# The last two token groups of the second mixture: 384 and 128 tokens in place of 256 and 256

## The chip, the cores and the metric

The kernel runs on one core of a Trainium2 chip. Its time is the device time in microseconds (us); a kernel's figure is the median of its runs. TensorE multiplies matrices, VectorE and ScalarE work on elements, GpSimd does some of that and issues gathers and scatters, and SyncE issues most transfers.

## The reference

A decaying linear attention (4 sequences of 768 tokens, 8 heads of 48) gives 3072 tokens of 384 numbers. A first mixture sends each token to one of 8 experts (384 to 1024 to 384). The second mixture, the part that changes, is this for all tokens:

```
h = np.maximum(np.maximum(x @ w1, x @ w2), x @ w3)   # 384 -> 768, three products
return (h @ w_out).astype(np.float32)                # 768 -> 384
```

## The kernel before

Attention comes first, ordered by a planner that is not touched. Then `experts` runs, with an order written out by hand: two loops over steps issue each engine's work in program order, and a table (`at`, `step`) attaches side work (loads, splits, gathers) to step numbers.

Products of the experts and of the second mixture are made with split numbers: each operand is a high part and a low part in the format fp32r, and `three` (lines 719 to 723) issues three products for one: high x high, high x low, low x high. Each is one TensorE instruction with its own load of 128 x 128 weights (the stationary operand), and the moving operand's columns stream through. The smallest number of columns that the kernel gives to such a product is 256.

The second mixture treats its 3072 tokens in groups of sizes `GS` (line 868): five of 512 and two of 256. `group(g)` splits a group's inputs into halves `gh` and `gl`. For each group there are NF = 6 steps, f = 0 to 5, one per 128 of the 768 hidden features:

- `up2(g, f)` makes the three products for 128 features: 3 weights x 3 slices of the inner dimension x 3 split products = 27 instructions, with the weights stationary and the group's G tokens as the moving columns. Each of the three results has a PSUM tile `pqt` of its own, out of four (pool `pq`). ScalarE copies the first into `h` (line 913), VectorE takes the maximum with the second and the third (914, 915), ScalarE makes the high part `hh` and VectorE the low part `hl` (`split`, lines 158 and 161).
- `down2(g, f)` multiplies by the output weights. Here the tokens are stationary, 128 at a time, and 384 output columns move: three instructions for each 128 tokens, added up over the six steps in a PSUM tile `pot` per 128 tokens. At f = 5 each such block is scaled by its gate (`sg`) out of PSUM into `orow`, by ScalarE for even blocks and by VectorE for odd ones, and GpSimd issues an indirect transfer that scatters the 128 rows to the output (line 941). The very last block of the program is halved: VectorE scales one half of its columns, ScalarE the other (lines 933 to 936).

`down2` of a step is issued after `up2` of the next step, so that the elementwise work between them has a whole `up2` to be done in. Only after the last `up2` nothing is left to put in between.

At step N1 + 37, in the last group, a matrix product and a copy make the flag (line 980) by which the program decides whether to run a slower path at the end; it is not taken here.

Of the kernel before, what the change touches and what calls it, by code (L numbers as in the profile page):

```python
# [10 lines left out]
F32 = mybir.dt.float32  # L11
# [3 lines left out]
AF = mybir.ActivationFunctionType  # L15
ALU = mybir.AluOpType
# [5 lines left out]
HD = H * D  # L22
# [132 lines left out]
def split(nc, hi, lo, src, hi_eng=None, lo_eng=None):  # L155

    if hi_eng is None:
        nc.scalar.copy(hi, src)  # L158
    else:
        hi_eng.tensor_copy(hi, src)  # L160
    (lo_eng or nc.vector).tensor_tensor(out=lo, in0=src, in1=hi.bitcast(F32), op=ALU.subtract)  # L161
# [427 lines left out]
def experts(ctx, tc, io, xs, R, ids_d, scale_d, V32):  # L589

    nc = tc.nc
# [12 lines left out]
    pq = ctx.enter_context(tc.tile_pool(name="pq", bufs=4, space=PSUM))  # L604
# [114 lines left out]
    def three(out, st_, mv, start, stop):  # L719
        (sh, sl), (mh, ml) = st_, mv  # L720
        nc.tensor.matmul(out, lhsT=sh, rhs=mh, start=start, stop=False)  # L721
        nc.tensor.matmul(out, lhsT=sh, rhs=ml, start=False, stop=False)  # L722
        nc.tensor.matmul(out, lhsT=sl, rhs=mh, start=False, stop=stop)  # L723

    HH = {}
    ACC = {}
# [14 lines left out]
    def down(e, f):  # L741
        if f == 0:
            ACC[e] = [po.tile([128, 512], F32, tag="po", name="pacc") for _ in range(3)]
        wh, wl = W[8 * e + f // 2 * 2 + 1]
        for m in range(3):
            ms = slice(m * 128, (m + 1) * 128)
            three(ACC[e][m][:, :CAPS[e]], (wh[:, f % 2, ms], wl[:, f % 2, ms]), HH[e, f], f == 0, f == 7)
        if f == 7:
            for m in range(3):
                o = yT[:, m, bass.ds(R["off"][e], CAPS[e]) if e else slice(CAP)]  # L750
                if m == 1:
                    nc.scalar.copy(o, ACC[e][m][:, :CAPS[e]])
                else:
                    nc.vector.tensor_copy(o, ACC[e][m][:, :CAPS[e]])
# [110 lines left out]
    xc.close()  # L865
    gp = ctx.enter_context(tc.tile_pool(name="gp", bufs=2))
    fp = ctx.enter_context(tc.tile_pool(name="fp", bufs=1))
    GS = [512] * 5 + [256] * 2
    G0 = [sum(GS[:g]) for g in range(len(GS))]
    XG = {}  # L870

    def group(g):
        G = GS[g]
        hi = gp.tile([128, 3, G], F32R, tag="gh", name="gh")
        lo = gp.tile([128, 3, G], F32R, tag="gl", name="gl")
        for k in range(3):
            split(nc, hi[:, k], lo[:, k], yT[:, k, G0[g]:G0[g] + G], lo_eng=nc.gpsimd if g else nc.vector)
        XG[g] = (hi, lo)

    group(0)  # L880
    down(*last)
    NG, NF = len(GS), F2 // 128
    ir = fp.tile([B * NC, 128], F32, name="ir", bufs=1)
# [8 lines left out]
    def places(g):  # L892
        for t in range(G0[g] // 128, (G0[g] + GS[g]) // 128):
            ic = gp.tile([128, 1], I32, tag="ic", name="ic", bufs=12)
            nc.vector.tensor_copy(ic, ig[:, t:t + 1])
            sg = gp.tile([128, 1], F32, tag="sg", name="sg", bufs=12)
            nc.gpsimd.indirect_dma_start(out=sg, out_offset=None, in_=scale_d, in_offset=bass.IndirectOffsetOnAxis(ap=ic[:, :1], axis=0),
                                         bounds_check=NT - 1, oob_is_err=False)
            R["ic", t], R["sg", t] = ic, sg

    def up2(g, f):
        G = GS[g]
        xh, xl = XG[g]
        fs = slice(f % 2 * 128, f % 2 * 128 + 128)
        pp = []
        for i in range(3):
            p = pq.tile([128, 512], F32, tag="pq", name="pqt")[:, :G]
            wh, wl = W[N1 + f // 2 * 4 + i]
            for k in range(3):
                three(p, (wh[:, k, fs], wl[:, k, fs]), (xh[:, k], xl[:, k]), k == 0, k == 2)  # L910
            pp.append(p)
        h = gp.tile([128, 512], F32, tag="h2", name="h2", bufs=2)[:, :G]
        nc.scalar.copy(h, pp[0])  # L913
        nc.vector.tensor_tensor(out=h, in0=h, in1=pp[1], op=ALU.max)  # L914
        nc.vector.tensor_tensor(out=h, in0=h, in1=pp[2], op=ALU.max)  # L915
        hi = hp.tile([128, 512], F32R, tag="hh", name="hh")[:, :G]
        lo = hp.tile([128, 512], F32R, tag="hl", name="hl")[:, :G]
        split(nc, hi, lo, h)
        HH[g, f] = (hi, lo)

    def down2(g, f):
        nt = GS[g] // 128
        if f == 0:
            ACC[g] = [po.tile([128, 512], F32, tag="po", name="pot") for _ in range(nt)]
        hh, hl = HH[g, f]
        wh, wl = W[N1 + f // 2 * 4 + 3]
        for t in range(nt):
            ts_ = slice(t * 128, (t + 1) * 128)
            three(ACC[g][t][:, :HD], (hh[:, ts_], hl[:, ts_]), (wh[:, f % 2], wl[:, f % 2]), f == 0, f == NF - 1)
            if f == NF - 1:  # L930
                o = gp.tile([128, HD], F32, tag="o", name="orow", bufs=4)
                n = G0[g] // 128 + t
                if t == GS[-1] // 128 - 1 and g == len(GS) - 1:
                    half = HD // 2
                    nc.vector.tensor_scalar(out=o[:, half:], in0=ACC[g][t][:, half:HD], scalar1=R["sg", n], scalar2=None, op0=ALU.mult)
                    nc.scalar.activation(out=o[:, :half], in_=ACC[g][t][:, :half], func=AF.Copy, scale=R["sg", n])
                elif t % 2:
                    nc.vector.tensor_scalar(out=o, in0=ACC[g][t][:, :HD], scalar1=R["sg", n], scalar2=None, op0=ALU.mult)
                else:
                    nc.scalar.activation(out=o, in_=ACC[g][t][:, :HD], func=AF.Copy, scale=R["sg", n])  # L940
                i = nc.gpsimd.indirect_dma_start(out=io["out"], out_offset=bass.IndirectOffsetOnAxis(ap=R["ic", n][:, :1], axis=0),  # L941
                                                 in_=o, in_offset=None, bounds_check=NT - 1, oob_is_err=False)
                tc.declare_no_dep(i.ins, group="rows", reason="each token has one row")
                tc.add_to_no_dep_group("rows", i.ins)
# [49 lines left out]
    for s in range(NG * NF):  # L994
        now = (s // NF, s % NF)
        up2(*now)
        if last:
            down2(*last)
        last = now
        step(N1 + s)  # L1000
    down2(*last)


# [160 lines left out]
def build(ctx, tc, io):  # L1164
# [26 lines left out]
    for e in range(E):  # L1191
        nc.gpsimd.memset(R["ec"][:, 0, e:e + 1], float(e))
    attention(tc, io["a"], io["qk"], io["v"], io, xs, R)
    experts(tc, io, xs, R, ids_d, scale_d, V32)
    flag = nc.values_load(R["flag"][0:1, 0:1], min_val=0, max_val=128, skip_runtime_bounds_check_because="a count of partitions")
    with tc.If(flag > 0):
# [71 lines left out]
```

## Time and profile before

| | |
|---|---|
| median of 3 runs | 809.87 us (808.35 to 811.32) |
| the profiled execution | 810.14 us |
| its span, first to last instruction | 808.3 us |
| mean granted clock of TensorE | 0.989 |
| TensorE products, weight loads (share of span) | 97%, 87% |
| VectorE, ScalarE, GpSimd | 59%, 49%, 34% |

The profile comes from one execution. A row of the timeline gives the start and the length in us, the engine, the line of the kernel, the operation, what it writes and reads, and in brackets how long the engine was idle before and what released it. PE is TensorE's products, PEld its weight loads, DVE VectorE, ACT ScalarE, POOL GpSimd. Products overlap in the pipeline: a record's length holds latency, so the spacing from one start to the next, and not the length, tells what a product costs in a row of them. Where a row stands for several instructions, its length goes from the first start to the last end. A plain fp32 product leaves two records for each product in the code.

### The profile page before, as it was taken

The page shows a single profiled execution, that of the slowest core. Times are in us where ns is not written, and L with a number is a line of the kernel's source. Part 1 is how long each engine was busy: PE and PEld are TensorE (multiplying, and loading weights), DVE is VectorE, ACT ScalarE, POOL GpSimd, SP SyncE. Part 2 cuts the span into 40 slices and gives each one's busy share as a digit, 9 for nine tenths or more (in the row PEclk, how much of TensorE's full clock was granted, in tenths as well). Part 3 has the DMA queues.
Part 4 walks back from the last instruction along what each step waited for, and adds up shares of the span by engine and source line. Part 5 has one row for each costly group of instructions (what it writes and reads, how often), then busy time and mean ns, then how long its engine had stood idle before and what let it go on. Part 6 is the DMA issues. An engine that isn't in the chain of part 4 may idle for free.

```text
span 808.3 us, 13655 instructions
## 1 busy us (share of the span) xinstructions
PE 784.1 (97%) x5131; PEld 699.9 (87%) x5131; DVE 479.9 (59%) x940; ACT 392.4 (49%) x638; POOL 272.6 (34%) x284
## 2 busy tenths in 40 slices
PE   8999999999996999999999999999999999999995
PEld 6778888888895888999999899888888888888994
DVE  3899999999773565766757543243433434334531
ACT  7989999997931444444445553111211112111211
POOL 1022144231212566655556871121312213112402
PEclk9999999999998999999999999999999999999998
DMA  7852533323115657557577751002102021020200
GB/s 242 262 183 93 165 126 123 128 97 115 56 47 150 210 172 243 193 179 242 192 231 242 245 176 60 1 1 97 59 17 83 0 98 59 20 78 1 99 21 23
DMA packets 59597, 97.63 MB, mean 121 GB/s; under 512 B 7141, under 2 KB 42885, under 8 KB 58501
## 3 DMA queue, kind: packets, MB, share of 16 engines
q1 hardware_dynamic: 55126, 86.96, 33.5%
q0 software_dynamic: 3904, 9.49, 3.1%
q8 instruction: 42, 0.69, 0.4%
q10 hardware_dynamic: 495, 0.25, 0.1%
q14 instruction: 30, 0.25, 0.1%
HBM read 79.64 MB, written 17.00 MB: 120 GB/s over the span
## 4 chain that ended last, share of the span: by engine, by line
PE 84%; issue 5%; DVE 4%; ACT 2%; DMA 2%; POOL 1%; SPq 1%; POOLq 0%; DVEq 0%; ACTq 0%
PE pqt L721 8%; PE pqt L723 8%; PE pqt L722 8%; PE pt L413 5%; PE pt L397 4%; PE php L721 4%; PE php L722 4%; PE php L723 4%; PE pacc L722 4%; PE pacc L723 4%; PE pacc L721 4%; PE ps L445 3%; PE pc L311 3%; PE ps L426 3%; PE pot L721 3%
## 5 line engine op out<-in xcount | busy, mean ns | idle before, releaser
L161 POOL TENSOR_TENSOR wl<-wraw,wh 128x768 fp32r<-128x768 f32 x68 | 132.1, 1950 | 82.8 <-ACT wh L158 72.8
L721 PE MATMUL pqt<-gh,wh 128*128 128x512 f32 (+1 forms) x378 | 136.9, 362 | 0.0
L722 PE MATMUL pqt<-gl,wh 128*128 128x512 f32 (+1 forms) x378 | 136.8, 362 | 0.0
L723 PE MATMUL pqt<-gh,wl 128*128 128x512 f32 (+1 forms) x378 | 136.8, 362 | 0.0
L158 ACT CAST hh<-h 128x512 fp32r<-128x512 f32 (+1 forms) x42 | 23.6, 561 | 153.8 <-DVE h L915 151.6
L914 DVE TENSOR_TENSOR h<-h,pqt 128x512 f32<-128x512 f32 (+1 forms) x42 | 25.7, 612 | 111.5 <-PE pqt L723 91.2
L737 ACT ACTIVATE hh<-php 128x480 fp32r<-128x480 f32 (+7 forms) x64 | 33.1, 517 | 100.5 <-PE php L723 100.3
L723 PEld LDWEIGHTS pqt<-gh,wl 128*128 128x128 f32 x378 | 70.9, 188 | 12.3
L721 PEld LDWEIGHTS pqt<-gh,wh 128*128 128x128 f32 x378 | 70.9, 188 | 11.1
L722 PEld LDWEIGHTS pqt<-gl,wh 128*128 128x128 f32 x378 | 70.9, 188 | 11.0
L738 DVE SCALAR_TENSOR_TENSOR hl<-php,hh 128x480 fp32r<-128x480 f32 (+7 forms) x64 | 37.4, 584 | 68.6 <-ACT hh L737 68.6
L721 PE MATMUL php<-xh,wh 128*128 128x480 f32 (+7 forms) x192 | 69.5, 362 | 0.0
L722 PE MATMUL php<-xl,wh 128*128 128x480 f32 (+7 forms) x192 | 67.7, 353 | 0.0
L723 PE MATMUL php<-xh,wl 128*128 128x480 f32 (+7 forms) x192 | 67.7, 352 | 0.0
L722 PE MATMUL pacc<-hl,wh 128*128 128x480 f32 (+7 forms) x192 | 67.3, 350 | 0.3 <-DVE hl L738 0.3
L723 PE MATMUL pacc<-hh,wl 128*128 128x480 f32 (+7 forms) x192 | 67.1, 350 | 0.0
L721 PE MATMUL pacc<-hh,wh 128*128 128x480 f32 (+7 forms) x192 | 67.0, 349 | 0.0
L158 ACT CAST wh<-wraw 128x768 fp32r<-128x768 f32 x76 | 61.9, 830 | 8.9 <-DMA wraw<-w 8.5
L913 ACT COPY h<-pqt 128x512 f32<-128x512 f32 (+1 forms) x42 | 22.1, 527 | 88.2 <-PE pqt L723 87.2
L941 POOL DMA_INDIRECT out<-orow,ic x24 | 23.8, 991 | 118.1 <-ACT orow L940 112.9
L511 POOL TENSOR_TENSOR run<-run,oh 128x8 bf16<-128x8 bf16 x24 | 9.9, 414 | 157.4 <-DVE oh L488 132.7
L915 DVE TENSOR_TENSOR h<-h,pqt 128x512 f32<-128x512 f32 (+1 forms) x42 | 25.7, 611 | 46.9 <-PE pqt L723 45.3
(168 smaller groups left out, 1833.1 us busy)
## 6 DMA issues: line engine op xcount, KB each, us to landing
wraw<-w SPq DMA_DIRECT2D x64, 384.0 KB
fa<-a SPq DMA_DIRECT2D x8, 1152.0 KB
a<-a SPq DMA_DIRECT2D x11, 768.0 KB
qk<-qk SPq DMA_DIRECT2D x11, 768.0 KB
raw<-v SPq DMA_DIRECT2D x9, 768.0 KB
v<-v SPq DMA_DIRECT2D x11, 512.0 KB
xe<-xs SPq DMA_DIRECT2D x21, 192.5 KB
v<-w SPq DMA_DIRECT2D x9, 384.0 KB
```

What stands on the lines that cost most here:

```text
L158: nc.scalar.copy(hi, src)
L161: (lo_eng or nc.vector).tensor_tensor(out=lo, in0=src, in1=hi.bitcast(F32), op=ALU.subtract)
L311: eng.matmul(d[name, j][:, :HD], lhsT=tri if name == "L" else trit, rhs=d["h" if name == "L" else "t"][:, j], start=True, stop=True)
L397: eng.transpose(d[p, j, g][:96, z * 128:(z + 1) * 128], d[yh, j][:, 4 * g + z].rearrange("p r n -> p (r n)"), idn)
L413: eng.matmul(p[:, z * 128:(z + 1) * 128], lhsT=d["kT", j][:, h], rhs=d["qT", j][:, h], start=True, stop=True)
L721: nc.tensor.matmul(out, lhsT=sh, rhs=mh, start=start, stop=False)
L722: nc.tensor.matmul(out, lhsT=sh, rhs=ml, start=False, stop=False)
L723: nc.tensor.matmul(out, lhsT=sl, rhs=mh, start=False, stop=stop)
L737: nc.scalar.activation(out=hi, in_=p, func=AF.Relu)
L738: nc.vector.scalar_tensor_tensor(out=lo, in0=p, scalar=0.0, in1=hi.bitcast(F32), op0=ALU.max, op1=ALU.subtract)
L914: nc.vector.tensor_tensor(out=h, in0=h, in1=pp[1], op=ALU.max)
L915: nc.vector.tensor_tensor(out=h, in0=h, in1=pp[2], op=ALU.max)
```

## The change

The last two groups have 384 and 128 tokens. In the group of 128, the three products of a step are put into one PSUM tile, side by side, 128 columns each. The last block, now the only one of its group, is scaled as a whole by VectorE; the halves are gone.

```diff
-    GS = [512] * 5 + [256] * 2
+    GS = [512] * 5 + [384, 128]
...
         pp = []
+        whole = pq.tile([128, 512], F32, tag="pq", name="pqt") if G == 128 else None
         for i in range(3):
-            p = pq.tile([128, 512], F32, tag="pq", name="pqt")[:, :G]
+            p = whole[:, i * G:(i + 1) * G] if G == 128 else pq.tile([128, 512], F32, tag="pq", name="pqt")[:, :G]
...
-                if t == GS[-1] // 128 - 1 and g == len(GS) - 1:
-                    half = HD // 2
-                    nc.vector.tensor_scalar(out=o[:, half:], in0=ACC[g][t][:, half:HD], scalar1=R["sg", n], scalar2=None, op0=ALU.mult)
-                    nc.scalar.activation(out=o[:, :half], in_=ACC[g][t][:, :half], func=AF.Copy, scale=R["sg", n])
-                elif t % 2:
+                if t % 2 or g == len(GS) - 1:
                     nc.vector.tensor_scalar(out=o, in0=ACC[g][t][:, :HD], scalar1=R["sg", n], scalar2=None, op0=ALU.mult)
```

## Rows read from the trace of the kernel before

**Rows 1.** The page: busy time by engine; the chain that ended last, by engine.
```profile
PE 784.1 (97%) x5131; PEld 699.9 (87%) x5131; DVE 479.9 (59%) x940; ACT 392.4 (49%) x638; POOL 272.6 (34%) x284
...
PE 84%; issue 5%; DVE 4%; ACT 2%; DMA 2%; POOL 1%; SPq 1%; POOLq 0%; DVEq 0%; ACTq 0%
```

**Rows 2.** Timeline, TensorE: a step of the last group (start us, length us).
```profile
784.57 0.28 PE L721 MATMUL pqt<-gh,wh 128*128 128x256 f32 x1
...
787.72 0.34 PE L721 MATMUL pot<-wh,hh 128*128 128x384 f32 x1
...
788.77 0.28 PE L721 MATMUL pqt<-gh,wh 128*128 128x256 f32 x1
```

**Rows 3.** Timeline, TensorE: the `down2` of a group of 512, first to next.
```profile
734.89 0.34 PE L721 MATMUL pot<-wh,hh 128*128 128x384 f32 x1
...
736.98 0.39 PE L721 MATMUL pqt<-gh,wh 128*128 128x512 f32 x1
```

**Rows 4.** Groups by shape, 640 us to the end: weight loads (busy us, mean ns).
```profile
L723 PEld LDWEIGHTS pqt<-gh,wl 128*128 128x128 f32 x220 | 41.3, 188 | 5.1
```

**Rows 5.** Groups by shape, whole span: products and a load of attention.
```profile
L413 PE MATMUL pt<-qT,kT 96*128 96x128 f32 x384 | 50.8, 280 | 0.0
...
L445 PE MATMUL ps<-v,kh 128*96 128x48 f32 x320 | 29.8, 246 | 0.0
...
L428 PEld LDWEIGHTS ps<-qT,S 96*64 96x64 f32 x320 | 23.1, 137 | 0.0
```

**Rows 6.** Timeline, TensorE: runs of such products (weights 96*128: rows x loaded columns).
```profile
30.96 1.48 PE L445 MATMUL ps<-v,kh 128*96 128x48 f32 x16
...
36.37 1.95 PE L413 MATMUL pt<-qT,kT 96*128 96x128 f32 x16
...
41.99 1.93 PE L471 MATMUL ps<-sel,yT 128*128 128x112 f32 x16
...
153.66 0.44 PE L426 MATMUL ps<-P,v 128*64 128x128 f32 x4
153.88 0.44 PE L428 MATMUL ps<-qT,S 96*64 96x128 f32 x4
```

**Rows 7.** Stretches: busy of PE, PEld, DVE, ACT, POOL; clock, DMA, GB/s.
```profile
157.00:158.90 1.90, 1.90 (x18) 1.90 (x17) 0.94 (x2) 1.90 (x5) 0.00 (x0) 1.00 0.90 323
...
784.57:788.77 4.20, 4.20 (x34) 4.20 (x34) 1.27 (x3) 0.78 (x3) 0.00 (x0) 1.00 0.01 4
```

**Rows 8.** Timeline, all engines: from the last product of `up2` on.
```profile
796.02 0.28 PE L723 MATMUL pqt<-gh,wl 128*128 128x256 f32 x1
...
796.34 0.42 DVE L915 TENSOR_TENSOR h<-h,pqt 128x256 f32<-128x256 f32 x1 [0.56 <-PE pqt L723]
...
797.25 0.44 PE L721 MATMUL pot<-wh,hh 128*128 128x384 f32 x1
...
797.71 0.45 PE L723 MATMUL pot<-wh,hl 128*128 128x384 f32 x1
...
798.20 0.58 ACT L940 ACTIVATE orow<-pot,sg 128x384 f32<-128x384 f32 x1 [1.00 <-PE pot L723]
...
798.72 0.42 DVE L935 TENSOR_SCALAR orow<-pot,sg 128x192 f32<-128x192 f32 x1 [1.06 <-PE pot L723]
799.05 1.01 POOL L941 DMA_INDIRECT out<-orow,ic  x1 [7.11 <-ACT orow L940]
799.17 0.42 ACT L936 ACTIVATE orow<-pot,sg 128x192 f32<-128x192 f32 x1 [0.39 <-DVE orow L935]
800.37 0.99 POOL L941 DMA_INDIRECT out<-orow,ic  x1 [0.30 <-issue]
```

**Rows 9.** Groups by shape, 640 us to the end: elementwise work (busy us, mean ns).
```profile
L914 DVE TENSOR_TENSOR h<-h,pqt 128x512 f32<-128x512 f32 x13 | 9.0, 689 | 40.5 <-PE pqt L723 32.5 <-issue 8.0
...
L913 ACT COPY h<-pqt 128x256 f32<-128x256 f32 x12 | 4.5, 373 | 14.9 <-PE pqt L723 13.8 <-issue 1.0
L938 DVE TENSOR_SCALAR orow<-pot,sg 128x384 f32<-128x384 f32 x7 | 4.1, 611 | 0.2 <-PE pot L723 0.2
```

## The prediction

> **What bounds the kernel now.** I read the engines' busy shares first, then the chain of waits, and both say one thing: TensorE is busy 97% of the span, and 84% of the chain that ended last is its work [rows 1]. So a change in the last stage is worth what it does to TensorE's spacing from one product to the next, plus what it does to the stretch after the last product, where nothing covers anything.
>
> Next the timeline of the last two groups. There a step (one `up2`, one `down2`) is 27 products of 256 columns and then 6 of 384. The 27 take 784.57 to 787.72, that is 3.15 us or 0.1167 each; the 6 take 1.05; the whole step is 4.20 [rows 2]. In the groups of 512 the 12 products of 384 columns take 734.89 to 736.98, 2.09 us or 0.1742 each [rows 3]. So a column costs 0.454 to 0.456 ns at 384 and at 256, and nothing fixed is seen. But every product loads its own 128 x 128 weights first (a load's record is 188 ns, part of it latency) [rows 4], and whether that load still hides under 128 columns is what this case turns on.
>
> **The rate at 128 columns.** The trace has no product of split numbers (fp32r) under 256 columns, so the nearest rows must bound it. In attention, plain fp32 products run with as few columns. 16 of `L471`, 112 columns with a 128-column load, take 1.93 us from first start to last end; with one record of 0.28 taken off, 15 spacings are 0.110 each. 16 of `L413`, 128 columns with a 128-column load, give (1.95 - 0.28) / 15 = 0.111. 16 of `L445`, only 48 columns but a 96-column load, give (1.48 - 0.246) / 15 = 0.082: far above 48 columns' worth, and 0.857 ns per loaded column, which for 128 gives 0.110. From four of `L426` to four of `L428`, whose loads have 64 columns, 0.22 goes by, so 0.055 each, again 0.86 ns per loaded column [rows 5, 6]. Load records shrink from 188 to 137 ns between 128 and 64 columns, 0.80 ns per column [rows 4, 5]. So loads seem to run one behind the other, at about 0.86 ns per column, and 128 columns of weights take 0.110 us however few columns follow. At 256 columns the stream (0.1167) just covers that; at 128 it does not.
> I bound the spacing x below by half of 0.1167 = 0.058 (columns alone) and above by two records of `L413`'s kind, 0.223: a small split product treated as a plain fp32 one, which in attention leaves two records (`scores` issues 192 products in all, 8 heads x 24 blocks, and `L413` shows 384 [rows 5]). I take 0.110, from the two rows with the same load.
>
> **The sum, part by part.**
> *Group of 384 for 256.* 6 steps x 27 = 162 products go from 0.1167 to 0.1742: 162 x 0.0575 = +9.3 us. The elementwise work grows by half, under a step that grows to (27 + 9) x 0.1742 = 6.27 us; ScalarE and VectorE use 0.8 and 1.3 us of a 4.2 us step now [rows 7], so it stays hidden. Uncovered, it would lengthen the way from a step's last maximum to its `down2`, which has a whole `up2` in between.
> *Group of 128 for 256.* 162 products go from 0.1167 to x: 162 x (0.110 - 0.1167) = -1.1 us. With x = 0.058 it would be -9.5, with 0.223 +17.2.
> *Products of `down2`.* 12 per pair of steps before (6 and 6) and after (9 and 3), same columns: 0. They need `hh` and `hl` of the step before; in the small group these come 1.6 and 1.9 us after the start of the last product of their step (worked out below), and 27 x 0.110 = 2.97 us of the next `up2` stand in between. At x = 0.058 that cover is 1.57 us and the 0.5 of an earlier `down2`: just enough.
> *One PSUM tile for three products.* Fewer buffers of `pq` are taken, which frees nothing, since TensorE waits for none now. What it can cost is that the copy of the first product, which now starts after 9 of the 27, must wait for all 27, because the tile that it reads is still being written. The row that bears on it: the two halves of the last scaling, VectorE's and ScalarE's, read one PSUM tile at different columns, and ScalarE's began at 799.17, when VectorE's (798.72 + 0.42) was done, its idle time put down to that [rows 8]. So I reckon with the wait. Queued behind the copy on ScalarE is only the cast of the same step, and behind that nobody but `down2` waits. In steps 0 to 4 the next `up2` hides it; in the last it is on the path.
> *The tail.* Before: the last product of `up2` starts at 796.02, VectorE's second maximum at 796.34; the first output product starts at 797.25, its third, which waits for `hl`, at 797.71; ScalarE's scaling at 798.20; GpSimd issues the two blocks of output rows at 799.05 and 800.37, the second late because the first holds the queue for 1.01 and 0.30 more goes by [rows 8]. After: operations of 128 columns. VectorE's 512-column maximum is 0.689 [rows 9] and its 256-column one 0.42 [rows 8], so 128 are 0.29; ScalarE's copy is 0.373 at 256 [rows 9], so about 0.26. I take 0.29 to 0.30 for cast and difference too, and 0.03 to 0.05 between two, as the rows show. From the start of the last product: its end 0.28, copy 0.32 to 0.58, maxima to 0.91 and 1.21, cast 1.24 to 1.54 (so `hh` is there at about 1.6), difference to 1.86, third output product at 1.92 with a record of 0.45, whole-row scaling on VectorE 2.41 to 3.02 (0.611 [rows 9]), and GpSimd's issue 0.27 behind it at 3.29, as 799.05 stands 0.27 behind 798.20 + 0.58. Before it was 800.37 - 796.02 = 4.35. So -1.1 us; from -0.4 (if the operations are no shorter than at 256 columns) to -1.7 (no wait for the shared tile). What follows the last issue, the rows' landing and the end of the program, is the same.
> *The rest.* Gathers of the scales and splits of `yT`: as many tokens, issued steps ahead, on GpSimd, which idles for whole steps [rows 7]: 0. The flag of the recurrence still comes two steps into the last group, now some 20 us before the end: 0.
>
> Sum: +9.3 - 1.1 - 1.1 = +7.1 us. The profiled execution took 810.14 (span 808.3 and 1.8 around it), so 817.2; the median of the runs shown is 0.27 lower, which makes 817.0. With x from 0.107 to 0.117 and the tail's bounds, 816 to 819.
>
> **Rivals.**
> *A, small split products lose their single pass.* The chip could run an fp32r product of 128 columns as it runs a plain one, in two records: x = 0.223, +9.3 + 17.2 - 1.1 = +25.4, 835.3. For it: no product of that format under 256 columns is in the trace to exclude it. Against it: the cost per column is the same from 384 to 256 [rows 2, 3], with no sign of a step.
> *B, the load hides after all (the other side: not slower).* If loads are pulled far enough ahead, x = 0.058: +9.3 - 9.5 - 1.1 = -1.3, 808.6, no change that can be told. The place is the spacing in the last six steps; it decides below x = 0.066, where 162 x (x - 0.0592) equals the tail's 1.1. For it: `L426` and `L428` do run 128 columns every 0.055. Against it: they load 64 columns, and `L445` shows that few columns do not speed up a wide load [rows 6].
> *C, something between.* If fp32r weights load faster than fp32 ones, and 128 columns come at the spacing that `L445` reaches with 96, 0.082: 162 x 0.0228 = +3.7 - 1.1 = +2.6, 812.5. For it: nothing but that the formats differ; against it: their records are as long (188 ns here; 0.110 and 0.111 at the two rows with a 128-column load). The Trainium skill has nearly that figure (TensorE: Matmul & The Clock Gate, "Back-to-back issue gap"): in a sustained stream of load and product pairs, about 81 ns for one of 128 columns. By that rule the time would be 812.3; `L413` and `L471`, at 0.111 and 0.110, do not agree with it, which is why it gets little.
> *D, the clock.* In the small group the array streams columns about half the time, and the granted clock may fall from 2.4 to 1.2 GHz. If all there took twice as long, x would be 0.22 and the time about 835. Against it: in attention's stretch of `L471`, just as bound by loads, the granted clock is 1.00 [rows 7].
>
> **How the numbers follow.** The forecast 0.63 (816 to 819), A 0.17, D 0.04, C 0.07, B 0.07, and 0.02 for a stall in the larger group's steps that I don't see. A measurement of this kernel can tell 0.3%, 2.4 us, from no change. Slower: forecast, A, D, the stall, and over half of C = 0.90; same: nearly all of B and the rest of C = 0.08; faster: 0.02. The range leaves out B and C and holds the rest: 814 to 837. The likeliest case's own is 816 to 819.
>
> **What would show it.** In the changed profile, the spacing of `pqt` in the last group: 0.110 is the forecast, 0.058 B, 0.082 C, 0.22 A or (at a lower granted clock) D. The weight loads there should stand end to end. A step of the group of 384 should take 6.27 us, one of the last 3.5. ScalarE's copy in the last group should start after the 27th product. From the last product's start to that group's only output issue: 3.3 us. The forecast is wrong if the last six steps take under 3 us each or over 4.

## The result, and the profile after

The changed kernel takes 819.34 us (817.47 to 821.21, 6 runs) against 810.37 (808.35 to 811.32, 6 runs) before: a ratio of 1.011, 95% interval 1.0092 to 1.0128, some 9 us slower. The prediction was 817.0, slower with a chance of 0.90. The profiled executions differ by a little less: 818.76 against 810.14 us, with spans of 817.0 and 808.3, 8.7 apart.

The first rows are the timeline of the changed kernel at its last small step (start us, length us, engine, line):

```profile
802.63 0.33 PE L723 MATMUL pot<-wh,hl 128*128 128x384 f32 x1
802.63 0.19 PEld L721 LDWEIGHTS pqt<-gh,wh 128*128 128x128 f32 x1
...
802.80 0.22 PE L721 MATMUL pqt<-gh,wh 128*128 128x128 f32 x1
802.80 0.19 PEld L722 LDWEIGHTS pqt<-gl,wh 128*128 128x128 f32 x1
802.86 0.27 PE L722 MATMUL pqt<-gl,wh 128*128 128x128 f32 x1
802.91 0.19 PEld L723 LDWEIGHTS pqt<-gh,wl 128*128 128x128 f32 x1
802.97 0.27 PE L723 MATMUL pqt<-gh,wl 128*128 128x128 f32 x1
803.02 0.19 PEld L721 LDWEIGHTS pqt<-gh,wh 128*128 128x128 f32 x1
803.08 0.28 PE L721 MATMUL pqt<-gh,wh 128*128 128x128 f32 x1
...
805.65 0.27 PE L723 MATMUL pqt<-gh,wl 128*128 128x128 f32 x1
```

These answer to [rows 2]. Loads start every 0.11 us, and each product starts about 0.06 behind its load's start, at the same pace. From 802.86 to 805.65 lie 25 spacings, 0.1116 each. At 256 columns it was 0.1167: half the columns, 4% less time. The very first spacing (802.80 to 802.86) is short: the load of the product at 802.80 had started at 802.63, together with the wide output product before it. The next wide product makes up for that, with a spacing of 0.23 in place of 0.17 (805.76 to 805.99 below).

The group of 384 on the same kernel's timeline: its very first product, then the products of its second step:

```profile
745.73 0.34 PE L721 MATMUL pqt<-gh,wh 128*128 128x384 f32 x1
...
752.49 0.34 PE L721 MATMUL pqt<-gh,wh 128*128 128x384 f32 x1
...
757.17 0.34 PE L721 MATMUL pot<-wh,hh 128*128 128x384 f32 x1
```

Its 27 products take 752.49 to 757.17, 4.68 (forecast 27 x 0.1742 = 4.70). And the tail, which answers to [rows 8]:

```profile
805.76 0.39 PE L721 MATMUL pot<-wh,hh 128*128 128x384 f32 x1
...
805.99 0.34 PE L722 MATMUL pot<-wl,hh 128*128 128x384 f32 x1
...
806.01 0.27 ACT L914 COPY h<-pqt 128x128 f32<-128x128 f32 x1 [2.30 <-PE pqt L723]
...
806.31 0.29 DVE L915 TENSOR_TENSOR h<-h,pqt 128x128 f32<-128x128 f32 x1 [2.27 <-ACT h L914]
806.63 0.29 DVE L916 TENSOR_TENSOR h<-h,pqt 128x128 f32<-128x128 f32 x1
806.95 0.30 ACT L158 CAST hh<-h 128x128 fp32r<-128x128 f32 x1 [0.67 <-DVE h L916]
807.29 0.29 DVE L161 TENSOR_TENSOR hl<-h,hh 128x128 fp32r<-128x128 f32 x1 [0.37 <-ACT hh L158]
...
807.31 0.45 PE L721 MATMUL pot<-wh,hh 128*128 128x384 f32 x1 [0.80 <-ACT hh L158]
...
808.14 0.62 DVE L935 TENSOR_SCALAR orow<-pot,sg 128x384 f32<-128x384 f32 x1 [0.56 <-PE pot L723]
809.04 0.99 POOL L938 DMA_INDIRECT out<-orow,ic  x1 [7.15 <-DVE orow L935]
```

The copy of the first product begins at 806.01, only after all 27, as forecast; from the last product (805.65) to the only issue (809.04) it is 3.39, in place of 4.35.

To put the 8.7 together, one row of the kernel before is needed that was not shown, the first product of its last two groups:

```profile
745.36 0.28 PE L721 MATMUL pqt<-gh,wh 128*128 128x256 f32 x1
```

| stretch | before | after | difference |
|---|---|---|---|
| start of span to the first product of the last two groups | 745.36 | 745.73 | +0.37, in work that did not change |
| from there to the last product of `up2` | 50.66 | 59.92 | +9.26 |
| from there to the last output issue | 4.35 | 3.39 | -0.96 |
| from there to the end | 7.93 | 7.96 | +0.03 |

The second and third rows together, "the stretch" below, are 55.01 before and 63.31 after. It is free of what differs from run to run in the earlier stages, so the experiments are read by it (in one profiled execution each) as well as by their times.

### The profile page after: what moved, and what is told of

It reads as the page before. It is cut to its first block, busy times and chain, and to the rows that moved or that the text cites. A ratio compares the mean times of both kernels' runs of the same rounds, so it can differ in the third digit from the quotient of the medians.

```text
span 817.0 us, 13641 instructions
## 1 busy us (share of the span) xinstructions
PE 792.3 (97%) x5131; PEld 707.9 (87%) x5131; DVE 480.2 (59%) x940; ACT 392.5 (48%) x637; POOL 272.9 (33%) x284
## 4 chain that ended last, share of the span: by engine, by line
PE 87%; DMA 5%; DVE 3%; issue 1%; SPq 1%; POOL 1%; ACT 0%; POOLq 0%; DVEq 0%; ACTq 0%
PE pqt L723 10%; PE pqt L722 10%; PE pqt L721 10%; PE pt L413 5%; PE php L721 4%; PE pt L397 4%; PE php L722 4%; PE php L723 4%; PE pacc L722 4%; PE pacc L723 4%; PE pacc L721 4%; PE pot L721 3%; PE pot L722 3%; PE pot L723 3%; PE pc L311 3%; PE ps L445 3%
## 5 line engine op out<-in xcount | busy, mean ns | idle before, releaser
L722 PE MATMUL pqt<-gl,wh 128*128 128x512 f32 (+2 forms) x378 | 139.6, 369 | 0.0
L723 PE MATMUL pqt<-gh,wl 128*128 128x512 f32 (+2 forms) x378 | 139.6, 369 | 0.0
L721 PE MATMUL pqt<-gh,wh 128*128 128x512 f32 (+2 forms) x378 | 139.4, 369 | 0.0
L915 DVE TENSOR_TENSOR h<-h,pqt 128x512 f32<-128x512 f32 (+2 forms) x42 | 25.7, 613 | 122.1 <-PE pqt L723 90.0
L158 ACT CAST hh<-h 128x512 fp32r<-128x512 f32 (+2 forms) x42 | 23.6, 562 | 151.3 <-DVE h L916 148.2
L914 ACT COPY h<-pqt 128x512 f32<-128x512 f32 (+2 forms) x42 | 22.2, 528 | 100.0 <-PE pqt L723 97.6
L916 DVE TENSOR_TENSOR h<-h,pqt 128x512 f32<-128x512 f32 (+2 forms) x42 | 25.7, 612 | 46.0 <-PE pqt L723 44.9
```

## The experiments

Two theories of the small group's spacing stand against each other. L: weight loads stand in line, 128 columns of weights take 0.11 us whatever streams. H: a small fp32r product streams at half rate, 128 columns in 0.1115. Both fit the changed kernel. A third, S, blames the shared PSUM tile. The first five experiments have a tile for each product. Code is shown in cuts, marked by `...`.

**A tile for each product.**

```diff
-        whole = pq.tile([128, 512], F32, tag="pq", name="pqt") if G == 128 else None
...
-            p = whole[:, i * G:(i + 1) * G] if G == 128 else pq.tile([128, 512], F32, tag="pq", name="pqt")[:, :G]
+            p = pq.tile([128, 512], F32, tag="pq", name="pqt")[:, :G]
```

> Each of the three products of the small group has a PSUM tile of its own again. Theory L (loads stand in line, about 0.11 us for 128 columns of weights): spacing of the small group's products stays 0.1115 and its steps 3.5 us. The shared tile's only cost is the late copy: now it starts after the 9th product, and from the last product's start to the last output issue it is 2.8 us instead of 3.4; time about 0.6 under the changed kernel's 819.3, so 818.7, a ratio of 1.010 to the kernel before. Rival S (sharing a tile is what slows the small group, by ordering writes and reads of one bank): steps fall to about 2.1 us (27 x 0.058 + 0.5), time about 810.

Measured: 817.16 us, ratio 1.0095 (1.0071 to 1.012); stretch 745.31 to 807.94, 62.63. Its timeline in the last step:

```profile
803.56 0.28 PE L723 MATMUL pqt<-gh,wl 128*128 128x128 f32 x1
803.59 0.27 ACT L913 COPY h<-pqt 128x128 f32<-128x128 f32 x1 [0.96 <-PE pqt L723]
...
805.23 0.27 PE L723 MATMUL pqt<-gh,wl 128*128 128x128 f32 x1
...
806.22 0.44 PE L721 MATMUL pot<-wh,hh 128*128 128x384 f32 x1
...
807.94 0.99 POOL L937 DMA_INDIRECT out<-orow,ic  x1 [7.16 <-DVE orow L934]
```

The copy now starts before the 27 are done, and the tail is 807.94 - 805.23 = 2.71 (forecast 2.8). From 803.56 to 805.23 the spacing is still 0.111 (15 products). S falls: sharing costs 0.68 us in the tail and nothing in the steps. By time alone this kernel and the changed one can't be told apart.

**Half the columns, the same loads.** 24 of each 27 products stream 64 columns; the last 64 tokens get only the first of the nine products of a result, and the other eight are left out for them.

```diff
...
+                    n = slice(0, 128 if k == 0 else 64)
+                    nc.tensor.matmul(p[:, n], lhsT=wh[:, k, fs], rhs=xh[:, k, n], start=k == 0, stop=False)
+                    nc.tensor.matmul(p[:, :64], lhsT=wh[:, k, fs], rhs=xl[:, k, :64], start=False, stop=False)
+                    nc.tensor.matmul(p[:, :64], lhsT=wl[:, k, fs], rhs=xh[:, k, :64], start=False, stop=k == 2)
...
```

> As e1_apart, but 24 of the 27 products of each small step stream 64 columns in place of 128 (the last 64 tokens get only the first of the nine products of a result). Theory L: spacing does not move, 0.110 to 0.112; steps 3.5 us; time as e1_apart within 0.5. Rival H (a small fp32r product streams at half the column rate, 128 columns in 0.1115): 64 columns in 0.056, 24 x 0.056 less per step, 7.7 us less in all, about 811.

Measured: 830.15 us, ratio 1.0243 (1.0217 to 1.0268); stretch 744.61 to 820.46, 75.85, which neither theory had. Two cuts of its timeline, and its stretches (busy us of PE, PEld, DVE, ACT, POOL; then the granted clock, DMA share, GB/s):

```profile
784.87 0.28 PE L912 MATMUL pqt<-gh,wh 128*128 128x64 f32 x1
784.98 0.28 PE L913 MATMUL pqt<-gl,wh 128*128 128x64 f32 x1
785.09 0.28 PE L914 MATMUL pqt<-gh,wl 128*128 128x64 f32 x1
785.20 0.28 PE L912 MATMUL pqt<-gh,wh 128*128 128x64 f32 x1
...
809.26 0.40 PE L912 MATMUL pqt<-gh,wh 128*128 128x64 f32 x1
809.48 0.40 PE L913 MATMUL pqt<-gl,wh 128*128 128x64 f32 x1
809.69 0.40 PE L914 MATMUL pqt<-gh,wl 128*128 128x64 f32 x1
809.90 0.40 PE L912 MATMUL pqt<-gh,wh 128*128 128x64 f32 x1
```

```profile
783.00:787.00 4.00, 4.00 (x33) 4.00 (x33) 1.58 (x11) 1.13 (x3) 0.00 (x0) 1.00 0.00 0
787.00:791.00 4.00, 4.00 (x33) 3.77 (x31) 1.09 (x4) 1.15 (x3) 2.98 (x3) 0.91 0.24 98
791.00:795.00 4.00, 4.00 (x21) 3.76 (x20) 0.41 (x2) 0.27 (x1) 0.00 (x0) 0.50 0.13 51
```

While the clock is granted in full, 64 columns go every 0.11 us, the same as 128: H falls, since it wants 0.056. Then, near 790, at the end of the second step of such products, the granted clock falls from 2.4 to 1.2 GHz and stays there, and the spacing becomes 0.213, nearly twice 0.111. So in this run the load, which sets the spacing, goes by TensorE's clock. L's time was wrong by 11.5 us all the same (830.15 against the 818.7 expected with 128 columns), for it had left the clock out.

**Half as many columns again.** 192 columns stream; the 64 tokens before the group are computed twice and dropped.

```diff
...
+    PAD = 64
...
-            p = whole[:, i * G:(i + 1) * G] if G == 128 else pq.tile([128, 512], F32, tag="pq", name="pqt")[:, :G]
+            M = G + PAD if G == 128 else G
+            p = pq.tile([128, 512], F32, tag="pq", name="pqt")[:, :M]
...
-            pp.append(p)
+            pp.append(p[:, M - G:])
```

> As e1_apart, but the small group's products stream 192 columns: the 64 tokens before it are computed a second time and dropped. Theory L: 192 columns at 0.4557 ns are 0.0875 us, still under the load, so spacing 0.1115 and no change in time beyond 0.5 us. Rival H: 192 columns at half rate are 0.167 us, 162 x 0.056 = +9 us, about 828.

Measured: 817.22 us, ratio 1.0095 (1.0073 to 1.0118); stretch 744.81 to 807.46, 62.65, against 62.63 with 128 columns. On its timeline:

```profile
783.35 0.28 PE L723 MATMUL pqt<-gh,wl 128*128 128x192 f32 x1
783.46 0.27 PE L721 MATMUL pqt<-gh,wh 128*128 128x192 f32 x1
783.57 0.28 PE L722 MATMUL pqt<-gl,wh 128*128 128x192 f32 x1
```

Half as many columns again are free, as L says.

**Half the load, the same columns.** 21 of each 27 products load 64 columns of weights; half of the hidden features get only two of their nine products, and the other seven are left out for them.

```diff
...
+                    cs = slice(fs.start, fs.start + 64)
+                    nc.tensor.matmul(p if k == 0 else p[:64], lhsT=wh[:, k, fs if k == 0 else cs], rhs=xh[:, k], start=k == 0, stop=False)
+                    nc.tensor.matmul(p[:64], lhsT=wh[:, k, cs], rhs=xl[:, k], start=False, stop=False)
+                    nc.tensor.matmul(p if k == 2 else p[:64], lhsT=wl[:, k, fs if k == 2 else cs], rhs=xh[:, k], start=False, stop=k == 2)
...
```

> As e1_apart, but 21 of the 27 products of each small step load 64 columns of weights in place of 128, with 128 columns streaming as before (half of the hidden features get only two of nine products). Theory L: those go at 0.055 to 0.060 (load and stream nearly equal), a step's 27 in 1.9 us in place of 2.97, 6.4 us less in all, about 812. Rival H: spacing stays 0.1115, time as e1_apart.

Measured: 810.70 us, ratio 1.0017 (1.0005 to 1.0029); stretch 744.53 to 800.69, 56.16, that is 6.47 less than with full loads (forecast 6.4). On its timeline (128*64: rows x loaded columns):

```profile
783.01 0.27 PE L914 MATMUL pqt<-gh,wl 128*128 128x128 f32 x1
783.11 0.28 PE L912 MATMUL pqt<-gh,wh 128*128 128x128 f32 x1
783.23 0.22 PE L913 MATMUL pqt<-gl,wh 128*64 128x128 f32 x1
783.29 0.22 PE L914 MATMUL pqt<-gh,wl 128*64 128x128 f32 x1
783.34 0.22 PE L912 MATMUL pqt<-gh,wh 128*64 128x128 f32 x1
783.40 0.22 PE L913 MATMUL pqt<-gl,wh 128*64 128x128 f32 x1
```

With a narrow load a product of 128 columns takes 0.06, with a full one 0.11. So a spacing is the longer of two times: a load of 128 columns, 0.1116 us (0.87 ns per loaded column), and the stream, 0.456 ns per column. A load of 64 columns takes 0.06 at most; how much less can't be seen here, since the stream of 128 columns takes as long.

**A third fewer loads.** High and low part of the small group's tokens stand side by side; one product of 256 columns with one load makes high x high and high x low, and their halves are added afterwards.

```diff
-                three(p, (wh[:, k, fs], wl[:, k, fs]), (xh[:, k], xl[:, k]), k == 0, k == 2)
+                    for a in ("big", "small") if k < 2 else ("small", "big"):
+                        if a == "big":
+                            nc.tensor.matmul(p, lhsT=wh[:, k, fs], rhs=XG[g, "both"][:, k], start=k == 0, stop=k == 2)
+                        else:
+                            nc.tensor.matmul(p[:, :G], lhsT=wl[:, k, fs], rhs=xh[:, k], start=False, stop=False)
...
+                nc.scalar.copy(s, pp[i][:, G:])
...
+                nc.vector.tensor_tensor(out=a, in0=s, in1=pp[i][:, :G], op=ALU.add)
```

> The small group only: high and low part of the tokens lie side by side, so that one product of 256 columns does high x high and high x low with one load, and their two halves are added afterwards (a copy and an addition more per result). 18 loads in place of 27 per step, the same columns. Theory L: a step's products take 9 x (0.1167 + 0.1115) = 2.05 us in place of 2.97, 5.5 less in all: from the first product of the group of 384 to the last output issue 57.1 to 58 us (62.6 with the tiles apart, 55.0 before the change), about 812 to 813, a ratio of 1.003 to the kernel before. Rival V: the additions make VectorE late (some 1.75 us of each 2.6 us step) and TensorE waits for hh, so that half of it or more is lost: over 60 us.

Measured: 811.86 us, ratio 1.0037 (1.0025 to 1.005); stretch 744.45 to 802.06, 57.61. A step's products on its timeline, and its tail:

```profile
794.17 0.28 PE L917 MATMUL pqt<-gh,wh 128*128 128x256 f32 x1
...
796.24 0.34 PE L721 MATMUL pot<-wh,hh 128*128 128x384 f32 x1
...
798.66 0.33 PE L917 MATMUL pqt<-gh,wh 128*128 128x256 f32 x1
...
802.06 0.99 POOL L957 DMA_INDIRECT out<-orow,ic  x1 [5.26 <-DVE orow L954]
```

The products take 2.07 (forecast 2.05). The same columns with two thirds of the loads give back 5.0 of the 7.6 us by which the tiles-apart kernel's stretch is behind the groups of 256, and V, the late additions, does not come as feared: before the tail the stretch is 5.7 us shorter, so the next step's work covers them. In the last step nothing does, and the tail is 3.40 (798.66 to 802.06) in place of 2.71. The kernel is still 2.6 behind the groups of 256.

**The small group first.** The changed kernel, shared tile and all, with `GS = [512] * 5 + [128, 384]`, and the last block scaled like the others.

> The changed kernel with the group of 128 before that of 384. Theory N (where the output products fall decides: those before the last product of up2 count in full, those behind it are partly covered): up to the last product 66 of them in place of 78, -2.1 us, and the tail is 5.9 in place of 3.4, because three blocks are issued 1.31 apart: from the first product of these groups to the last output issue 63.8 (63.3 changed), time within 1 us of 819. Rival T (the prediction's count: the output products cost the same wherever they stand): the tail alone counts, +2.5, 65.9, near 822.

Measured: 818.98 us, ratio 1.0125 (1.011 to 1.0141); stretch 744.53 to 808.44, 63.91. Its tail on the timeline:

```profile
802.35 0.34 PE L723 MATMUL pqt<-gh,wl 128*128 128x384 f32 x1
...
805.82 1.01 POOL L938 DMA_INDIRECT out<-orow,ic  x1 [9.89 <-ACT orow L937]
...
807.14 1.00 POOL L938 DMA_INDIRECT out<-orow,ic  x1 [0.30 <-issue]
808.44 0.98 POOL L938 DMA_INDIRECT out<-orow,ic  x1 [0.30 <-issue]
```

The tail is 6.09, 2.70 longer than in the changed kernel, and the part before it 57.82, 2.10 shorter. N holds (63.8 forecast), T falls (65.9).

**Six groups of 512.** The kernel before with `GS = [512] * 6`; the product that makes the flag moves into the last step.

> The kernel before with six groups of 512, no small ones (the flag's product moved into the last two steps). Theory N: up2 costs the same per column; 60 output products before the last product of up2 in place of 72, -2.1; the tail from there to the last issue 7.8 in place of 4.35, because four blocks are issued 1.31 apart: from the first product of the last 512 tokens to the last issue 56.4 in place of 55.0, a time 1.4 above before. Rival T: +3.5, 58.5.

Measured: 810.75 us, ratio 1.002 (1.0011 to 1.003); stretch 744.10 to 800.17, 56.07 (N 56.4, T 58.5). No group is below 256 columns, and nothing is lost to loads; in all the stretch is 1.1 us longer than before the change. Its tail, with four blocks to scatter, is 8.11 (792.06 to 800.17) in place of 4.35, and the part before it 2.70 shorter, 2.1 of that for 12 output products fewer.

## Why the prediction was right, and where it was short

- *The rate at 128 columns*: 0.110 forecast, 0.1116 measured. It was taken from plain fp32 rows with the same load [rows 6], and the runs with 64 and 192 columns and with narrow loads show that it is the load. A (two passes, 0.223), B (load hidden, 0.058) and C (0.082) are out by that number, and with 64-column products the spacing stays 0.11, so columns can't be what sets it. A step of the group of 384 took 6.25 us (752.49 to 758.74; forecast 6.27), one of the last 3.54 (3.5). The Trainium skill's 81 ns for a pair at 128 columns (TensorE: Matmul & The Clock Gate, "Back-to-back issue gap") does not hold for these fp32r products, at 0.1116; its rule for loads in the section "LDWEIGHTS (loading the stationary operand)", columns over 1.2 GHz whatever the number of rows, gives an estimate of 0.107, near what is measured at full clock, but in the run where the clock fell the spacing went to 0.213, so here it is no fixed rate.
- *Group of 384*: 6 x (4.68 - 3.15) = +9.2, forecast +9.3. *Group of 128*: 162 x (0.1116 - 0.1167) = -0.8, forecast -1.1.
- *Products of `down2`*: this step failed. The prediction put them at 0, because a pair of steps has 12 before and after. But `down2` runs a step late. Before the change 72 output products stand between the first product of these groups and the last of `up2` (12 of the group of 512, 6 x 6, then 4 x 6), and 12 behind it, partly under the elementwise work; after it 78 (12, 6 x 9, 4 x 3) and 6. Six products moved from the covered tail to the path: 6 x 0.1742 = +1.05. The tail's gain had been counted with fewer products in it, and the other side of that entry was forgotten. The swapped groups show it the other way round: 66 in place of 78, 2.10 less.
- *The tail*: -1.1 forecast, -0.96 measured. The wait of the copy for all 27 was there and costs 0.68, against 0.6 allowed. The row that the prediction took it from did not show it, though: the two halves of the last scaling also write one tile `orow` [rows 8], so the second may have waited for that tile. The run with a tile for each product is what shows the wait.
- *Sum*: +9.2 - 0.8 + 1.05 - 0.96 = +8.5 against +8.3 in the stretch; the 0.4 that the span has beyond that lies ahead of the changed work.
- *D, the clock*: it did not fall at 128 columns, and it did at 64. A stretch of the changed kernel and one of the kernel with tiles apart, columns as above:

```profile
799.26:802.80 3.54, 3.54 (x32) 3.54 (x31) 0.93 (x5) 0.57 (x2) 1.05 (x1) 1.00 0.01 0
```

```profile
799.00:803.00 4.00, 4.00 (x37) 4.00 (x36) 1.23 (x5) 0.65 (x3) 1.04 (x1) 1.00 0.01 0
```

  So the clock can fall in such a stream, and in these two stretches it did not. The argument against it was thin: attention's stretch at 1.00 [rows 7] is 1.90 us long, and the run with 64 columns, too, had 1.00 for longer than that, from the first product of its small group at 782.61 to near 790, before the clock fell. That D stayed away is in part luck.

The range, 814 to 837, held the time; its upper part came from A and D, neither of which happened. What was too narrow was the likeliest case's own, 816 to 819.

## What to carry to other kernels

A product costs the longer of its stream and the next load: with 128 x 128 weights in fp32r, here, 64, 128 and 192 columns all take 0.111 us, and 256 take 0.1167. By an estimate from these figures the two times meet at 245 columns (0.1116 over 0.456 ns); nothing between 192 and 256 was run. A last group below that size saves nothing on these products; there, fewer loads (two moving operands side by side under one load) give back what shorter streams can't, here 5.0 of 7.6 us. And where a loop runs one stage late, count what stands before and behind the last product, not per step: work moved out of a covered tail is new work.

## What the runs showed of the hardware that was not expected

- A dense stream of products with 64 columns under 128-column loads lost the granted clock, 1.00 to 0.50 near 790, in its second step, though by its records a product was in flight all the time (PE busy 4.00 of 4.00 us); the same stream with 128 columns kept it. Why it fell is not shown. Half the columns made the kernel 13 us slower (830.15 against 817.16).
- With the clock at half, the spacing of load-bound products doubled too, 0.11 to 0.213: in this run loads went by the granted clock.
- A short product behind a wide one is followed by the next after 0.06, and the next wide one is late by as much (0.23 in place of 0.17): at the change from one kind of product to the other a cost is shifted and none is lost.
